# The ninth key block's low-half score term, made over the full array and ahead of the side-by-side pair

## The chip, the cores and the metric

The kernel runs on one core of a Trainium2 chip. The metric is the device time of one launch in microseconds, and a kernel's time is the median of several launches. The engines are named as the profile names them: PE is the matrix engine (PEld its weight loads, which can lie beside its matmuls), DVE the vector engine, ACT the scalar engine, POOL the general-purpose engine, and SP the engine that issues the DMAs. PSUM is the memory into which PE writes its sums.

## The reference

An attention whose queries are averaged in twos feeds a two-layer network. It is cut here to what matters:

```python
# q, k, v: (4, 8, 1152, 64); w_in: (512, 2048); w_out: (2048, 512)
q_pool = q.reshape(B, H, S // 2, 2, D).mean(axis=3)        # 576 queries a head
scores = 1 / sqrt(D) * q_pool @ k.transpose(0, 1, 3, 2)    # 576 x 1152
attn = softmax(scores)
a = attn @ v
x = a.transpose(0, 2, 1, 3).reshape(B * S // 2, H * D)     # 2304 x 512
h = x @ w_in
out = where(h > 0, h, exp(min(h, 0)) - 1) @ w_out          # 2304 x 512, float32
```

## The kernel before, in words

All products are made on PE in half precision, with every operand split into a high half and a low half, so that a product is a sum of terms: high by high, high by low, low by high.

The work goes by batch, and in a batch by four pairs of heads. A pair's queries come in nine steps: four tiles of 128 queries for each of the two heads, and one last step in which the 64 queries that are left of each head stand together (`st.h is None`). That makes 4 x 4 x 9 = 144 steps, 128 of the first kind and 16 of the last.

A step begins with its scores (`scores()`, lines 712 to 733): 128 queries against 1152 keys, written to the one PSUM buffer `s` of three banks. The keys of a head lie in `kT` as nine blocks of 128. In a block the partitions hold 64 rows of the one half of the keys and 64 rows of the other; in the even blocks of the first head the high half lies below, in the odd ones above, and in the second head the other way round. `keys[h]` groups them: entry 0 is four blocks (512 columns) with the high half in partitions 0 to 63, entry 1 is four blocks with the high half in partitions 64 to 127, and entry 2 is the ninth block alone (128 columns). The queries lie in `qT`: index 0 has the high half in both sets of 64 partitions, index 1 the low half in both sets.

The first three matmuls (line 721) take the high half of the queries against all 128 partitions, that is against both halves of the keys: 512, 512 and 128 columns. The next three (line 730) take the low half of the queries against the high half of the keys, and so use 64 rows of the array each: entry 0 on rows 0 to 63 and entry 1 on rows 64 to 127, which stand next to each other in the order and run side by side (the pair), and then the ninth block alone, on the 64 rows where its high half lies. In a last step each of the six is there twice, once for each head, with 64 query columns.

After the scores, DVE scales them, copies them out of PSUM and takes the smallest of each row (`biggest`, line 736); ACT takes the exponential (line 742); a reciprocal, the high half of the weights (line 761 on ACT or 753 on POOL) and their low half (line 756 on DVE) follow; a transposing DMA makes `pT` (line 781); and PE multiplies it with the values (lines 819 and 825). Since there is one buffer `s`, the first score matmul of a step waits until line 736 of the step before has read it.

Beside this run the splitting of inputs and weights and the network, whose matmuls are lines 933 and 1000. What stands where on an engine is set by a planner in the kernel (`Plan.run`), which goes through all tasks with a written price and a due time for each. The scores are one task with a written price of 950 (1100 for a last step); what the function does inside is not seen by the planner.

The low half of the queries is put into `qT` by two DMAs (`q_lo`, line 525), one for each set of 64 partitions; the copy of the high half into the upper set (`q_hi`, line 528) is a task that follows them, and the scores follow `q_hi`.

Of the kernel before, what the change touches and what calls it, by code (L numbers as in the profile page):

```python
# [226 lines left out]
def attention_moe_kernel(  # L227
# [9 lines left out]
    nc = tc.nc  # L237
# [85 lines left out]
    for b, s0, nt, lo in [(b, 0, 4, True) for b in range(0, B)]:  # L323
# [6 lines left out]
        while t0 < u.n:  # L330
            n = 256 if u.n - t0 != 320 else 320
# [6 lines left out]
    for u in units:  # L338
# [3 lines left out]
        for p in range(NP):  # L342
            pr = Rec()
# [345 lines left out]
    r = plan.add("DVE", 150.0, 0.0, wo_top, wo_max)  # L689
# [12 lines left out]
    def attention(st):  # L702
        u, pr = st.u, st.pr
        t0 = st.t0
        s, nm, ep = (plan.buf(*x) for x in (("s",), ("nm",), ETAGS[u.i]))
# [6 lines left out]
        def scores():  # L712
            jobs = [(h, slice(64 * h, 64 * h + 64)) for h in range(2)] if st.h is None else [(st.h, slice(0, 128))]
            j = 2 * u.nt if st.h is None else st.t + st.h * u.nt
            keys = {}
            for h, rows in jobs:
                kt = pr.kT.ap[:, h]
                keys[h] = [kt[:, h:8:2], kt[:, 1 - h:8:2], kt[:, 8:9]]
            for c, n in enumerate((512, 512, 128)):
                for h, rows in jobs:  # L720
                    nc.tensor.matmul(  # L721
                        s.ap[rows, c, 0:n], pr.qT.ap[:, 0, j, rows], keys[h][c],
                        start=True, stop=False, skip_group_check=True,
                    )
            for cs in ((0, 1), (2,)):
                for h, rows in jobs:
                    for c in cs:
                        r0, n = ((0, 512), (64, 512), (64 * h, 128))[c]
                        r = slice(r0, r0 + 64)
                        nc.tensor.matmul(  # L730
                            s.ap[rows, c, 0:n], pr.qT.ap[r, 1, j, rows], keys[h][c][r],
                            start=False, stop=True, skip_group_check=True,
                        )

        def biggest():
            nc.vector.tensor_scalar(  # L736
# [42 lines left out]
        def ptr():  # L779
            nc.sync.dma_start_transpose(  # L780
                out=pT.ap[:, :, half * 128:half * 128 + 128], in_=ep.ap[:, 0:2 * S]
            )

        ts_ = plan.add("PE", 950.0 if st.h is not None else 1100.0, t0 - K("KS", u), scores, pr.kdone + [pr.qs], [s, pr.kT, pr.qT])
        tm = plan.add("DVE", 1345.0, t0 - K("KM", u), biggest, [ts_, pr.sc], [s, nm, ep, pr.sm])
        te = plan.add("ACT", 1255.0, t0 - K("KE", u), expo, [tm], [nm, ep])
# [59 lines left out]
        n = 256 if st.h is not None else 128  # L846
# [217 lines left out]
```

## Time and profile before

| what | value |
|---|---|
| median of three runs | 947.41 us |
| lowest and highest run | 945.33 and 953.8 us |
| the profiled execution, its own time | 947.0 us |
| its span, first to last instruction | 945.2 us |
| mean granted clock of PE in it | 0.899 of full speed |
| busy PE, DVE, ACT, POOL | 740.6, 728.4, 691.2, 370.6 us |

The span is what the rows of the trace can explain; 1.8 us of the profiled execution lie around it. An engine's busy time is the time in which at least one of its instructions ran. Matmuls are pipelined: one starts while the one before it is still in the array, so what one costs the engine is the distance between starts, and its recorded length is longer. The ends of matmuls are modelled.

### The profile page before, as it was taken

Reading aid. Unit: us, or ns where it says so; the run is one execution under the profiler, and the core shown is the slowest. Engines: PE = TensorE matmul, PEld = TensorE weight load, DVE = VectorE, ACT = ScalarE, POOL = GpSimd, SP = SyncE. Lnnn points to the kernel's source line nnn. Section 1 sums busy time; section 2 is a strip of 40 time slices with the busy share of each in tenths; the row PEclk is TensorE's granted clock in tenths of the full one; section 3 lists DMA queues with packets and bytes.
Section 4 is the critical chain, followed back from the end, with each engine's and each line's share of the span. In section 5 each row is a group of like instructions: output and inputs, shape, how many; then the busy total and the mean of one; then the engine's idle time right before and its main releaser. Section 6 shows DMA issues by size and latency. Waiting matters only on the chain.

```text
span 945.2 us, 14736 instructions
## 1 busy us (share of the span) xinstructions
PE 740.6 (78%) x5283; PEld 420.6 (44%) x5283; DVE 728.4 (77%) x1235; ACT 691.2 (73%) x1169; POOL 370.6 (39%) x344
## 2 busy tenths in 40 slices
PE   0256555566939898988997989769979899789997
PEld 0123232233716455445644544338436544366563
DVE  5998999989898878867785897877877897785220
ACT  4587868878778879767777997568877987675360
POOL 3420513101737757402623772226324852034260
PEclk9998656657959999999998989989989999789999
DMA  7899999999948679897598989886799889754000
GB/s 235 221 211 199 232 224 250 237 188 263 224 95 182 133 166 207 153 185 125 110 186 183 196 172 208 160 160 105 158 212 202 170 157 173 133 100 76 23 1 28
DMA packets 434056, 156.94 MB, mean 166 GB/s; under 512 B 395840, under 2 KB 414272, under 8 KB 433984
## 3 DMA queue, kind: packets, MB, share of 16 engines
q1 hardware_dynamic: 433984, 156.01, 79.6%
q8 instruction: 41, 0.67, 0.3%
q14 instruction: 31, 0.25, 0.1%
HBM read 45.09 MB, written 4.72 MB: 53 GB/s over the span
## 4 chain that ended last, share of the span: by engine, by line
PE 28%; DVE 17%; DMA 14%; ACT 7%; issue 6%; POOL 5%; SPq 1%; DVEq 0%; POOLq 0%; ACTq 0%
DMA pT<-ep 11%; PE r L933 11%; PE r L1000 9%; DVE ep L736 6%; DVE ep L756 5%; PE r L819 3%; ACT ep L742 3%; PE s L721 2%; PE r L825 2%; POOL g L972 2%; PE s L730 1%; DMA kT<-kn 1%; DVE x L842 1%; ACT ep L761 1%; ACT tmp L944 1%
## 5 line engine op out<-in xcount | busy, mean ns | idle before, releaser
L756 DVE SCALAR_TENSOR_TENSOR ep<-ep,nm 128x1152 f16<-128x1152 f32 x132 | 209.7, 1593 | 18.1 <-ACT ep L761 10.5
L742 ACT ACTIVATE ep<-ep,nm 128x1152 f32<-128x1152 f32 x132 | 165.2, 1251 | 77.4 <-DVE ep L736 57.9
L736 DVE TENSOR_SCALAR_CACHE_REDUCE ep<-s,sm 128x1152 f32<-128x1152 f32 x132 | 186.3, 1411 | 40.6 <-DMA pT<-ep 25.7
L933 PE MATMUL r<-x,wi 128*128 128x256 f16 (+1 forms) x1536 | 204.1, 293 | 8.1 <-DVE x L842 4.2
L721 PE MATMUL s<-kT,qT 128*128 128x512 f16 (+3 forms) x480 | 108.8, 368 | 90.8 <-DVE ep L736 71.3
L933 PEld LDWEIGHTS <-wi 128*128 128x128 f16 x1536 | 150.5, 100 | 58.4 <-issue 18.3
L1000 PE MATMUL r<-wo,g 128*128 128x512 f16 (+1 forms) x864 | 174.4, 380 | 0.0
L761 ACT ACTIVATE ep<-ep,nm 128x1152 f16<-128x1152 f32 x111 | 138.3, 1247 | 23.7 <-DVE nm L750 23.3
L819 PE MATMUL r<-pT,v 128*128 128x256 f16 (+1 forms) x855 | 107.3, 281 | 31.1 <-DMA pT<-ep 16.5
L1000 PEld LDWEIGHTS <-g 128*128 128x128 f16 (+1 forms) x864 | 73.1, 100 | 87.9 <-issue 9.3
L949 POOL TENSOR_SCALAR tmp<-tmp,us 128x320 f32<-128x320 f32 (+1 forms) x96 | 73.2, 765 | 93.3 <-ACT tmp L944 92.9
L721 PEld LDWEIGHTS <-qT 128*128 128x128 f16 (+1 forms) x480 | 40.8, 105 | 144.5 <-issue 113.6
L819 PEld LDWEIGHTS <-v 128*128 128x128 f16 x864 | 72.5, 108 | 62.6 <-issue 33.1
L954 DVE SCALAR_TENSOR_TENSOR tmp<-r,wk,tmp 128x320 f32<-128x320 f32 (+1 forms) x96 | 57.5, 611 | 31.0 <-POOL tmp L949 30.6
L753 POOL TENSOR_SCALAR ep<-ep,nm 128x1152 f16<-128x1152 f32 x21 | 29.2, 1392 | 128.7 <-DVE nm L750 127.3
L972 POOL TENSOR_TENSOR g<-tmp,g 128x320 f16<-128x320 f32 (+1 forms) x70 | 72.1, 1036 | 12.0 <-ACT g L968 10.4
L730 PE MATMUL s<-kT,qT 64*128 64x512 f16 (+3 forms) x480 | 72.2, 369 | 0.0
L825 PE MATMUL r<-pT,v 128*64 128x256 f16 (+1 forms) x855 | 67.6, 282 | 0.0
L384 POOL TENSOR_SCALAR q<-q,sm 128x576 f32<-128x576 f32 x14 | 12.6, 897 | 134.6 <-ACT qn L429 119.2
L941 ACT ACTIVATE tmp<-r 128x320 f32<-128x320 f32 (+1 forms) x96 | 46.5, 485 | 24.4 <-PE r L933 19.6
L944 ACT ACTIVATE tmp<-tmp,us 128x320 f32<-128x320 f32 (+1 forms) x96 | 58.0, 608 | 1.3
L837 ACT ACTIVATE x<-r,sm 64x256 f32<-64x256 f32 (+1 forms) x96 | 39.8, 414 | 23.7 <-PE r L825 22.3
(123 smaller groups left out, 960.1 us busy)
## 6 DMA issues: line engine op xcount, KB each, us to landing
k<-in_k_dram SPq DMA_DIRECT2D x16, 576.0 KB, 5.0
v<-in_v_dram SPq DMA_DIRECT2D x16, 576.0 KB, 4.6
q<-in_q_dram SPq DMA_DIRECT2D x32, 256.0 KB, 3.4
qT<-qT SPq DMA_DIRECT2D x48, 144.0 KB, 2.8
g<-in_moe_w_in_dram SPq DMA_DIRECT2D x13, 512.0 KB, 5.6
g<-in_moe_w_out_dram SPq DMA_DIRECT2D x13, 512.0 KB, 5.2
out_dram<-tmp SPq DMA_DIRECT2D x16, 256.0 KB, 2.8
pT<-ep SPq DMA_TRANSPOSE x130, 4.8
```

The costliest lines, as they stand in the source:

```text
L721: nc.tensor.matmul(s.ap[rows, c, 0:n], pr.qT.ap[:, 0, j, rows], keys[h][c], start=True, stop=False, skip_group_check=True,)
L730: nc.tensor.matmul(s.ap[rows, c, 0:n], pr.qT.ap[r, 1, j, rows], keys[h][c][r], start=False, stop=True, skip_group_check=True,)
L736: nc.vector.tensor_scalar(e_(), s.ap.rearrange("p a b -> p (a b)")[:, 0:S], pr.sm.ap[:, 12:13], None, op0=ALU.mult, op1=ALU.min, accum_out ...
L742: nc.scalar.activation(out=e_(), in_=e_(), func=AF.Exp, bias=nm.ap[:, 0:1], scale=-1.0, accum_out=nm.ap[:, 2:3],)
L756: nc.vector.scalar_tensor_tensor(out=p_(1), in0=e_(), scalar=nm.ap[:, 3:4], in1=p_(0), op0=ALU.mult, op1=ALU.subtract)
L761: nc.scalar.activation(out=p_(0), in_=e_(), func=AF.Copy, scale=nm.ap[:, 3:4])
L819: nc.tensor.matmul(x.ap[:, os], vt[:, order[c]].rearrange("p e d -> p (e d)"), pT.ap[:, c, cs], start=(c == 0), stop=False, skip_group_che ...
L825: nc.tensor.matmul(x.ap[r0:r0 + 64, os], vt[:, order[c], 0], pT.ap[:, NCH + c, cs], start=False, stop=(c >= NCH - 2), skip_group_check=True,)
L933: nc.tensor.matmul(hp.ap[:, f * n:(f + 1) * n], w[:, a, c, (f0 + f) * 128:(f0 + f + 1) * 128], x16.ap[:, e, c, g0:g0 + n], start=(i == 0), ...
L949: nc.gpsimd.tensor_scalar(en.ap[:, :m], en.ap[:, :m], -1.0, us.ap[:, 5:6], op0=ALU.add, op1=ALU.mult)
L972: nc.gpsimd.tensor_tensor(out=l, in0=gv, in1=h, op=ALU.subtract)
L1000: nc.tensor.matmul(op.ap[r0:r0 + tn, :], gt[qd].ap[:, a, fi, o:o + tn], w_out16(f // 2)[:, e, f % 2, :], start=(i < 128 // tn), stop=(i >= ...
```

## The change

The ninth block's low-half term is taken out of the set of 64-row matmuls. It is now made over all 128 partitions, with the low half of the queries against both halves of the keys, and it stands between the three high-half matmuls and the pair. The term low by low is added by it for the ninth block alone. The pair is now the last of the group.

```diff
-            for cs in ((0, 1), (2,)):
-                for h, rows in jobs:
-                    for c in cs:
-                        r0, n = ((0, 512), (64, 512), (64 * h, 128))[c]
-                        r = slice(r0, r0 + 64)
-                        nc.tensor.matmul(
-                            s.ap[rows, c, 0:n], pr.qT.ap[r, 1, j, rows], keys[h][c][r],
-                            start=False, stop=True, skip_group_check=True,
-                        )
+            for h, rows in jobs:
+                nc.tensor.matmul(
+                    s.ap[rows, 2, 0:128], pr.qT.ap[:, 1, j, rows], keys[h][2],
+                    start=False, stop=True, skip_group_check=True,
+                )
+            for h, rows in jobs:
+                for c in range(2):
+                    r = slice(64 * c, 64 * c + 64)
+                    nc.tensor.matmul(
+                        s.ap[rows, c, 0:512], pr.qT.ap[r, 1, j, rows], keys[h][c][r],
+                        start=False, stop=True, skip_group_check=True,
+                    )
```

In the changed file the moved matmul is line 726 and the pair is line 733; later lines stand three further down (1000 is 1003).

On PE, a group in the middle of the run that a matmul of the second layer follows. `LDWEIGHTS` is a weight load, `MATMUL` names result, moving operand and weights, and the size at the end is that of the result. First before:

```order
L721 MATMUL s_3613<-kT_2455,qT_2444 128x128
L730 LDWEIGHTS qT_2444
L730 MATMUL s_3613<-kT_2455,qT_2444 128x512
L730 LDWEIGHTS qT_2444
L730 MATMUL s_3613<-kT_2455,qT_2444 128x512
L730 LDWEIGHTS qT_2444
L730 MATMUL s_3613<-kT_2455,qT_2444 128x128
L1000 LDWEIGHTS g_3017
L1000 MATMUL r_3385<-wo_1503,g_3017 128x512
```

The same place after:

```order
L721 MATMUL s_3613<-kT_2455,qT_2444 128x128
L726 LDWEIGHTS qT_2444
L726 MATMUL s_3613<-kT_2455,qT_2444 128x128
L733 LDWEIGHTS qT_2444
L733 MATMUL s_3613<-kT_2455,qT_2444 128x512
L733 LDWEIGHTS qT_2444
L733 MATMUL s_3613<-kT_2455,qT_2444 128x512
L1003 LDWEIGHTS g_3017
L1003 MATMUL r_3385<-wo_1503,g_3017 128x512
```

The 128-column matmul of the low half went from behind the pair to ahead of it; as many loads and matmuls as before stand there, and what precedes and follows the group is the same.

On PE, the first group of a pair of heads, with the semaphores on which an instruction waits (DMAHW4 and DMAHW5 belong to the two DMAs of `q_lo`). Before:

```order
L721 MATMUL s_228<-kT_169,qT_159 128x128
L730 LDWEIGHTS qT_159 [waits DMAHW4_49]
L730 MATMUL s_228<-kT_169,qT_159 128x512
L730 LDWEIGHTS qT_159 [waits DMAHW5_49]
L730 MATMUL s_228<-kT_169,qT_159 128x512
```

After:

```order
L721 MATMUL s_228<-kT_169,qT_159 128x128
L726 LDWEIGHTS qT_159 [waits DMAHW5_49,DMAHW4_49]
L726 MATMUL s_228<-kT_169,qT_159 128x128
L733 LDWEIGHTS qT_159
L733 MATMUL s_228<-kT_169,qT_159 128x512
```

Both waits now stand at the load of the moved matmul. On DVE, ACT, POOL and SP the order and the waits are the same in both kernels, and on PE nothing outside the groups moved.

## Rows read from the trace of the kernel before

**Rows 1.** The page's busy time, and the chain that ended last by engine and line.

```profile
PE 740.6 (78%) x5283; PEld 420.6 (44%) x5283; DVE 728.4 (77%) x1235; ACT 691.2 (73%) x1169; POOL 370.6 (39%) x344
...
PE 28%; DVE 17%; DMA 14%; ACT 7%; issue 6%; POOL 5%; SPq 1%; DVEq 0%; POOLq 0%; ACTq 0%
...
by line: DMA pT<-ep 10.6%; PE r L933 10.6%; PE r L1000 9.1%; issue 6.3%; DVE ep L736 5.5%; DVE ep L756 4.7%; PE r L819 2.9%; ACT ep L742 2.7%; PE s L721 2.3%; PE r L825 1.7%; POOL g L972 1.6%; PE s L730 1.4%; DMA kT<-kn 0.9%; DVE x L842 0.9
```

**Rows 2.** The page's costliest groups: busy us, mean ns | idle before, releaser.

```profile
L736 DVE TENSOR_SCALAR_CACHE_REDUCE ep<-s,sm 128x1152 f32<-128x1152 f32 x132 | 186.3, 1411 | 40.6 <-DMA pT<-ep 25.7
...
L721 PE MATMUL s<-kT,qT 128*128 128x512 f16 (+3 forms) x480 | 108.8, 368 | 90.8 <-DVE ep L736 71.3
...
L721 PEld LDWEIGHTS <-qT 128*128 128x128 f16 (+1 forms) x480 | 40.8, 105 | 144.5 <-issue 113.6
...
L730 PE MATMUL s<-kT,qT 64*128 64x512 f16 (+3 forms) x480 | 72.2, 369 | 0.0
```

**Rows 3.** The waits, whole span: us in total, times, longest us.

```profile
PE s L721 <- DVE ep L736: 71.3, 47, 10.8
...
PEld L730 <- issue: 45.1, 144, 0.5
...
DVE ep L736 <- PE s L730: 10.8, 12, 2.0
```

**Rows 4.** Timeline of PE, one group at full clock: start us, length us, instruction.

```profile
404.11 0.38 PE L721 MATMUL s<-kT,qT 128*128 128x512 f16 x1 [0.47 <-DVE ep L736]
404.32 0.38 PE L721 MATMUL s<-kT,qT 128*128 128x512 f16 x1
404.54 0.22 PE L721 MATMUL s<-kT,qT 128*128 128x128 f16 x1
404.69 0.39 PE L730 MATMUL s<-kT,qT 64*128 64x512 f16 x2
404.92 0.22 PE L730 MATMUL s<-kT,qT 64*128 64x128 f16 x1
405.06 0.39 PE L1000 MATMUL r<-wo,g 128*128 128x512 f16 x1
```

**Rows 5.** Timeline of PE, one full-array stream of 64 columns, and its weight loads.

```profile
257.56 0.44 PE L819 MATMUL r<-pT,v 128*128 128x64 f16 x9
257.92 0.34 PE L825 MATMUL r<-pT,v 128*64 128x64 f16 x9
...
257.56 0.32 PEld L819 LDWEIGHTS <-v 128*128 128x128 f16 x9
```

**Rows 6.** Timeline of PE: two side-by-side 512-column matmuls, then one over the full array.

```profile
423.05 0.38 PE L1000 MATMUL r<-wo,g 128*64 128x512 f16 x2
423.36 0.39 PE L721 MATMUL s<-kT,qT 128*128 128x512 f16 x1
```

**Rows 7.** Timeline of PE, the end of one last step's group.

```profile
417.53 0.41 PE L730 MATMUL s<-kT,qT 64*64 64x512 f16 x4
417.77 0.23 PE L730 MATMUL s<-kT,qT 64*64 64x128 f16 x2
417.93 0.28 PE L819 MATMUL r<-pT,v 128*128 128x256 f16 x1
```

**Rows 8.** Timeline of PE, the end of a group at half clock.

```profile
410.84 0.31 PE L721 MATMUL s<-kT,qT 128*128 128x128 f16 x1
411.08 0.61 PE L730 MATMUL s<-kT,qT 64*128 64x512 f16 x2
411.48 0.31 PE L730 MATMUL s<-kT,qT 64*128 64x128 f16 x1
411.73 0.39 PE L819 MATMUL r<-pT,v 128*128 128x256 f16 x1
```

**Rows 9.** Stretches of rows 4 and 8: busy by engine, then PE's granted clock, DMA.

```profile
404.10:405.06 0.96, 0.95 (x6) 0.31 (x6) 0.96 (x1) 0.96 (x1) 0.00 (x0) 1.00 1.37 157
410.03:411.73 1.70, 1.70 (x7) 0.39 (x6) 1.29 (x2) 1.62 (x3) 0.00 (x0) 0.50 0.65 122
```

## The prediction

> **What bounds the kernel now.** I read first the busy times: PE, DVE and ACT are each busy for about three quarters of the span and none is full, so no single engine sets the end [rows 1]. Then the chain that ended last: it runs through PE for 28% of the span, DVE 17%, DMA 14%, ACT 7%. The reader should look there for the lines that the change touches: score lines 721 and 730 hold 2.3% and 1.4%, together 3.7% of 945.2 us, or 35 us [rows 1]. Both lines together are busy for 108.8 + 72.2 = 181 us [rows 2]. So about a fifth (35 / 181 = 0.19) of the time in the score matmuls lies on the path that sets the end. That fifth is what I multiply PE's savings by, since in the other groups PE waits anyway: the waits show PE's line 721 standing 71.3 us for the DVE copy that frees the one PSUM buffer [rows 3]. In the other direction DVE's line 736 stands for the end of the low-half matmuls only 12 times, for 10.8 us in all [rows 3].
>
> Next comes the timeline of one group, because the whole change lies inside it. At full clock (granted 1.00 there [rows 9]) the starts are: two high-half matmuls of 512 columns at 404.11 and 404.32, the high half of the ninth block at 404.54, the pair at 404.69, the ninth block's low half at 404.92, and the second layer at 405.06 [rows 4]. Distances between starts are what counts. A 512-column matmul costs 0.215, so 128 columns should cost a quarter, 0.054. But from the 128-column matmul to the pair it is 0.15, and from the last 128-column matmul to the next full-array one 0.14. So going from the full array to 64 rows, and coming back, costs about 0.09 each time, on top of the columns.
>
> **The change part by part.** Loads and matmuls are as many as before, with the same numbers of columns: per group 512, 512, 128, a pair of 512, and 128. Entry into 64 rows and return from it happen once each, before and after. What moves is the second 128.
>
> Removed, per group of the first kind at full clock: the stretch from the pair to the short matmul (404.69 to 404.92, 0.23) and from it to the next work (0.14), together 0.37 [rows 4].
>
> Added: (a) a second full-array matmul of 128 columns behind the first. No row shows two in a row. Its price is bounded from below by 0.03: nine full-array matmuls of 64 columns have their loads within 0.32 us, and with the last load's own length of some 0.105 taken off, eight steps take 0.215 [rows 2, 5]. It is bounded from above by 0.15, the step at which the array changes its shape [rows 4]. I take 0.055, the quarter of a 512, since the 64-column stream shows that a full-array matmul with a load of its own is spaced by its columns. (b) The way from the pair straight to the next full-array work. No row shows that either; the nearest is two side-by-side 512s, split in columns of the array rather than in rows, followed by a full-array matmul: 423.05 to 423.36, 0.31 [rows 6]. The lower bound is 0.215, a return that costs nothing; the upper one 0.215 + 0.14 = 0.36, the columns plus the whole of today's last step. I take 0.31.
>
> Sum per group: 0.055 + 0.31 - 0.37 = about -0.005 us, which is within the rounding. In a last step, from the pairs to the short ones 0.24 and on to the next work 0.16 [rows 7], 0.40 in all, against 0.055 + 0.31 and 0.01 for the second head's start, is -0.02. At half clock (0.50 [rows 9]) it is 0.24 into the pair, 0.40 to the short matmul, 0.25 to the next work: 0.89 [rows 8]. Afterwards it is 0.11 for the second 128, 0.24, and then 0.40 or 0.43 (twice 0.215) with a return of 0.14 (0.25 less 0.11): 0.89 to 0.92, so 0.00 to +0.03 slower; I take +0.015. With two clock levels and a mean granted clock of 0.899, PE is at the lower for (1 - 0.899) / 0.5 = 20% of the time, hence about 29 of 144 groups. All together: 102 x -0.005 - 13 x 0.02 + 29 x 0.015 = -0.3 us of PE time, of which a fifth is on the path: **-0.1 us**.
>
> The release of DVE is the other thing that moves: `biggest` starts on the last matmul of the group, which was a short one and is now the second of the pair. Before: pair to short 0.23, and 0.22 for the short one's length, 0.45 behind the pair's start. After: the pair starts 0.055 later and lasts 0.39, 0.445 [rows 4]. The ends are modelled, so the difference of 0.005 is none; a matmul's columns plus its way through the array are the same in either order. So the loop of scores and copy does not get shorter.
>
> The waits for the two DMAs of the low half of the queries now both stand at the load of the moved matmul, and queued behind it are the pair and all of PE. In the trace of before the loads of line 730 never waited for a DMA, only for "issue" (45.1 us in 144 groups [rows 3]), and the first score matmul, ahead of them, already waits for a task that follows these two DMAs. I cost the merged wait at nothing; if its cover were gone, it would be 16 waits, one for each pair of heads.
>
> Other engines and queues keep their order, so nothing else moves but by these hundredths.
>
> **Bounds.** With both unknown prices at their upper ends a group costs 0.095 + 0.05 - 0.005 = +0.14, or 20 us of PE in 144 groups and 4 us on the path: 951.0. With both at the lower ends it costs -0.025 - 0.095 - 0.005 = -0.125, or -18 us and -3.6 us on the path: 943.4.
>
> **The rivals.** Slower: the load of the moved matmul is not hidden. The load of a full set of weights is recorded at 105 ns on average [rows 2], longer than the 54 ns of the 128-column matmul ahead of it, whereas it stands behind a pair of 512 today. If the second short matmul had to wait for its load, each group would cost 0.105 - 0.055 = +0.05 us, 7.2 us of PE, **948.4** with a fifth on the path and 954.2 with every group on it. Against it speak the 64-column matmuls, spaced at under 0.03 with loads just as long [rows 5]. It decides from the point where the two short starts lie more than 0.055 apart; over 1% it would need 0.066 per group and all groups on the path.
> The Trainium skill's page "TensorE: Matmul & The Clock Gate", section "LDWEIGHTS (loading the stationary operand)", speaks for this rival: a load takes as many nanoseconds as it has columns over 1.2, about 107 for a full set. By that as a spacing the sum would be the 948.4 above; the recorded length agrees, the spacing in rows 5 does not, so I keep this as a rival.
>
> Faster: the return from the pair costs nothing, because the next full-array work enters behind a long pair rather than behind a short matmul. Then each group saves 0.095, 13.7 us of PE, **944.3** with a fifth on the path, and over 1% faster only where 70% of the groups were on it. Against it speaks the 0.31 behind the side-by-side 512s, which has 0.095 over its columns [rows 6].
>
> Clock: the low half of the ninth block uses 128 rows instead of 64, and PE might be granted the full clock more often. If all of the fifth that runs at half clock went to full, half of 20% of PE's busy 740.6 us, 74 us, would go, 28% of it on the path, 21 us: **926**. The columns that go through PE and its gaps stay the same, so I see no ground for it.
>
> **How the numbers follow.** The forecast is the profiled execution's 947.0 us less 0.1; that execution lies 0.4 us under the median of 947.41, so **947.0** serves for both. Its chance is 0.81; the slower rival gets 0.09, the faster 0.07, the clock 0.03. The bounds of the prices give 943.4 to 951.0. The same program's runs lie from 945.33 to 953.8, two of the three within 2.1 us, so I widen each end by about 1: 942.5 to 952.0, which takes in the first two rivals as priced. A change of under 1% is about what a measurement of this kernel cannot tell from none. Over 1% faster takes most of the clock rival and the far end of the faster one, 0.05; over 1% slower the far end of the slower one and a clock that turns the other way, 0.05; within 1% is left with 0.90.
>
> **What would show it.** In the timeline of the changed kernel at full clock: the moved matmul 0.05 to 0.06 behind the ninth block's high half; the pair 0.15 behind that; the next full-array work 0.31 behind the pair. A distance of 0.10 between the short ones shows the load; 0.22 behind the pair shows a free return. The wait of DVE's line 736 for the score matmuls should stay near 11 us in a dozen times, the mean granted clock near 0.90, and the moved matmul's load should not wait for a DMA. The forecast is wrong if more than a fifth of the groups are on the path, or if shifts of hundredths change which transposing DMA is late, which no row here prices.

## The result, and the profile after

The changed kernel takes 940.9 us in the median (938.42 to 945.23, 10 runs), the kernel before on the same chip 950.72 us (942.96 to 953.8, 10 runs). The ratio is 0.9915, with a 95% interval from 0.989 to 0.994: faster by 0.85%, some 8 us. That is inside the band of 1% that got most of the chance, but the time is 1.6 us below the low end of the range, and the forecast of -0.1 us is not what happened.

The two profiled executions stand 947.0 against 944.64 us, so only 2.4 of the 8 us lie between them: the one of before is 3.7 us under its median here, the one after 3.7 us above its own. What they show well is the inside of a group, what stands where, and the time from the 45th group on, where traces of one kernel agree (table at the end of the experiments).

The page of the changed kernel, span, busy time and chain by engine:

```profile
span 942.8 us, 14748 instructions
...
PE 733.5 (78%) x5283; PEld 428.9 (45%) x5283; DVE 730.5 (77%) x1235; ACT 690.6 (73%) x1169; POOL 370.0 (39%) x344
...
PE 25%; DVE 17%; DMA 14%; ACT 8%; issue 7%; POOL 6%; SPq 2%; DVEq 0%; POOLq 0%; ACTq 0%
```

They answer to [rows 1]. As many matmuls as before, but twelve instructions more than the 14736 of before. PE's busy time is 7.1 us smaller.

The page's groups after (the copy is now line 739, the pair 733), which answer to [rows 2]:

```profile
L739 DVE TENSOR_SCALAR_CACHE_REDUCE ep<-s,sm 128x1152 f32<-128x1152 f32 x132 | 186.4, 1412 | 40.8 <-DMA pT<-ep 28.0
...
L721 PE MATMUL s<-kT,qT 128*128 128x512 f16 (+3 forms) x480 | 108.7, 368 | 91.9 <-DVE ep L739 73.6
```

The waits after, as in [rows 3]:

```profile
PE s L721 <- DVE ep L739: 73.6, 47, 10.8
...
DVE ep L739 <- PE s L733: 7.9, 9, 2.4
```

Neither the copy nor the score matmuls wait noticeably more or less. The timeline of PE after, for the group of [rows 4] from its second matmul on:

```profile
408.21 0.38 PE L721 MATMUL s<-kT,qT 128*128 128x512 f16 x1
408.42 0.22 PE L721 MATMUL s<-kT,qT 128*128 128x128 f16 x1
408.48 0.22 PE L726 MATMUL s<-kT,qT 128*128 128x128 f16 x1
408.63 0.39 PE L733 MATMUL s<-kT,qT 64*128 64x512 f16 x2
408.95 0.39 PE L1003 MATMUL r<-wo,g 128*128 128x512 f16 x1
```

The second 128 follows 0.06 behind the first (forecast 0.055), the pair 0.15 behind that (0.15), the next work 0.32 behind the pair (0.31). With these, a group costs 0.06 + 0.32 - 0.37 = +0.01 us. At half clock, by the starts of such groups in the same trace, the three distances are 0.11, 0.25 and 0.54, together about the 0.89 of before. A last step ends so, against [rows 7]:

```profile
417.91 0.22 PE L726 MATMUL s<-kT,qT 128*64 128x128 f16 x2
418.07 0.41 PE L733 MATMUL s<-kT,qT 64*64 64x512 f16 x4
418.41 0.28 PE L822 MATMUL r<-pT,v 128*128 128x256 f16 x1
```

So the groups are what was forecast, and the 8 us do not come from their length. The one other thing that the trace shows at the moved line is the twelve instructions:

```profile
L726 PEldq EVENT_SEMAPHORE  x12: 51/51/51, 39.2 to 783.5; - x12
```

These are instructions of 51 ns each in PE's queue, at loads where two waits now stand together; the order listed them as part of the load.

### The profile page after: what moved, and what is told of

The parts are those of the page before. It is cut to its first block, busy times and chain, and to the rows that moved or that the text cites. A ratio compares the mean times of both kernels' runs of the same rounds, so it can differ in the third digit from the quotient of the medians.

```text
span 942.8 us, 14748 instructions
## 1 busy us (share of the span) xinstructions
PE 733.5 (78%) x5283; PEld 428.9 (45%) x5283; DVE 730.5 (77%) x1235; ACT 690.6 (73%) x1169; POOL 370.0 (39%) x344
## 4 chain that ended last, share of the span: by engine, by line
PE 25%; DVE 17%; DMA 14%; ACT 8%; issue 7%; POOL 6%; SPq 2%; DVEq 0%; POOLq 0%; ACTq 0%
DMA pT<-ep 11%; PE r L936 9%; PE r L1003 8%; DVE ep L739 5%; DVE ep L759 4%; PE r L822 3%; ACT ep L745 3%; PE s L721 2%; PE r L828 2%; POOL g L975 1%; ACT ep L764 1%; DMA q<-in_q_dram 1%; PE s L733 1%; DMA kT<-kn 1%; DVE x L845 1%
## 5 line engine op out<-in xcount | busy, mean ns | idle before, releaser
L936 PE MATMUL r<-x,wi 128*128 128x256 f16 (+1 forms) x1536 | 200.6, 289 | 8.8 <-DVE x L845 4.8
L936 PEld LDWEIGHTS <-wi 128*128 128x128 f16 x1536 | 148.6, 99 | 55.5 <-issue 17.6
L822 PE MATMUL r<-pT,v 128*128 128x256 f16 (+1 forms) x855 | 104.8, 276 | 32.2 <-DMA pT<-ep 12.4
L828 PE MATMUL r<-pT,v 128*64 128x256 f16 (+1 forms) x855 | 65.7, 276 | 0.0
L733 PE MATMUL s<-kT,qT 64*128 64x512 f16 (+1 forms) x320 | 62.6, 435 | 0.0
L840 ACT ACTIVATE x<-r,sm 64x256 f32<-64x256 f32 (+1 forms) x96 | 39.8, 415 | 20.9 <-PE r L828 19.3
```

Source lines behind the costliest of these rows:

```text
L733: nc.tensor.matmul(s.ap[rows, c, 0:512], pr.qT.ap[r, 1, j, rows], keys[h][c][r], start=False, stop=True, skip_group_check=True,)
L822: nc.tensor.matmul(x.ap[:, os], vt[:, order[c]].rearrange("p e d -> p (e d)"), pT.ap[:, c, cs], start=(c == 0), stop=False, skip_group_che ...
L828: nc.tensor.matmul(x.ap[r0:r0 + 64, os], vt[:, order[c], 0], pT.ap[:, NCH + c, cs], start=False, stop=(c >= NCH - 2), skip_group_check=True,)
L936: nc.tensor.matmul(hp.ap[:, f * n:(f + 1) * n], w[:, a, c, (f0 + f) * 128:(f0 + f + 1) * 128], x16.ap[:, e, c, g0:g0 + n], start=(i == 0), ...
```

## The experiments

Ratios are to runs of the kernel before on the same chip, with 95% intervals; each kernel has 6 to 12 runs. The clock is the granted clock, the median of a kernel's runs.

**First four: the row count or the order?** At first I looked at the clock. In the trace after, PE was granted half clock for less time in the middle of the run, and the ten runs showed 0.902 to 0.918 against the 0.899 of the profile before. So one theory was that a short matmul over all 128 rows keeps PE at its full level; a rival, that the order does it; a third, that any small shift reshuffles the run.

*c_before*, the kernel before unchanged.

> The kernel before, unchanged, as a control. Every theory expects the ratio to the kernel before at 1.000 with the interval across it, a median near 950 us. What it gives is the granted clock of each of its runs: the clock theory (the short matmul over all 128 rows keeps PE at its full level for more of the time) expects 0.895 to 0.901 here, against 0.902 to 0.918 in the ten runs of the changed kernel. The theory that only the order counts, and the theory that any shift of hundredths reshuffles the run, expect no such separation, or none that goes with the time.

Measured: 0.9989 (0.9962 to 1.0016), 949.46 us, clock 0.900, from 0.890 to 0.907.

*e_full_last*, the short matmul over 128 rows, behind the pair:

```diff
-            (short matmul over 128 rows)
             (pair)
+            (short matmul over 128 rows)
```

> The short low-half matmul over all 128 rows, but behind the pair, where it stood before. Clock theory: the gain stays, ratio 0.988 to 0.995, clock 0.904 to 0.915. Order theory (what counts is that the pair is last and the short matmul ahead of it): no gain, ratio 0.997 to 1.003. Reshuffling theory: anything from 0.988 to 1.005, without relation to the clock. By starts alone the group should be as long as in the changed kernel, within 0.01 us.

Measured: 0.9978 (0.9958 to 0.9998), 949.3 us, clock 0.904.

*e_short64_first*, the short matmul ahead of the pair, on 64 rows:

```diff
+                r = slice(64 * h, 64 * h + 64)
-                    s.ap[rows, 2, 0:128], pr.qT.ap[:, 1, j, rows], keys[h][2],
+                    s.ap[rows, 2, 0:128], pr.qT.ap[r, 1, j, rows], keys[h][2][r],
```

> The short low-half matmul ahead of the pair, but on 64 rows as before, without the second key half. Order theory: the gain stays, ratio 0.988 to 0.995. Clock theory: no gain, ratio 0.997 to 1.003, clock near 0.90. Reshuffling theory: anything from 0.988 to 1.005. By starts alone the group is shorter by about 0.05 us, since the short matmul lies in the same shape of the array as the pair and its rows may run beside it.

Measured: 0.9998 (0.9976 to 1.0021), 950.87 us, clock 0.899.

*c_after*, the changed kernel again.

> The changed kernel once more, as a control on this chip: ratio 0.989 to 0.994 by every theory, clock 0.902 to 0.918.

Measured: 0.9916 (0.9894 to 0.9938), 943.31 us, clock 0.906.

The gain repeats, and neither half of the change has it. The order alone gives nothing. The full rows alone raise the clock by 0.004 and give at most 0.4%, so the clock theory as I had put it fell, unless a later release of DVE had eaten its gain in *e_full_last*.

**Next four: the merged wait, the clock, the release.** What only the changed kernel had was the pair of waits at one load.

*e_first_new*, the new form only in the first step of each pair of heads:

```diff
+            if st is pr.steps[0]:
+                (short matmul over 128 rows, then the pair)
+            else:
+                (the old three)
```

> The new form of the group in the first step of each pair of heads only (16 of 144 groups), the old form elsewhere. These 16 groups are those in which the two waits for the copies of the low half stand at one load. Wait theory (the merged wait, with the twelve extra semaphore instructions that it brought, moved the time): the whole gain, ratio 0.989 to 0.995. Clock theory (a short matmul over 128 rows in every group keeps PE longer at its full level): a ninth of the gain, 0.998 to 1.001, clock 0.898 to 0.902.

Measured: 0.9969 (0.9948 to 0.999), 946.32 us, clock 0.8985; 14748 instructions.

*e_first_old*, the same with the two branches exchanged.

> The complement: the old form in the first step of each pair, the new one in the other 128 groups. The waits stand as in the kernel before. Wait theory: no gain, 0.998 to 1.002. Clock theory: eight ninths of the gain, 0.990 to 0.995, clock 0.904 to 0.910.

Measured: 1.001 (0.9985 to 1.0034), 948.84 us, clock 0.905; 14736 instructions.

*e_old_fullextra*, one more short matmul over 128 rows:

```diff
+            for h, rows in jobs:
+                nc.tensor.matmul(
+                    s.ap[rows, 2, 128:256], pr.qT.ap[:, 0, j, rows], keys[h][2],
+                    start=True, stop=True, skip_group_check=True,
+                )
             for cs in ((0, 1), (2,)):
```

> The group of the kernel before, and one more matmul over 128 rows and 128 columns ahead of the pair, into columns of the buffer that nothing reads. The group and the release of DVE become about 0.055 us later, and the pair is not last. Clock theory: the clock rises to 0.904 to 0.912, half-clock time between 290 and 815 us falls from 41 to 51 to about 30 us, and the time falls in spite of the longer group, ratio 0.991 to 0.998. Theory that it takes the order and the rows together for another reason (what follows the pair): no gain, or a loss of 0.055 x 144 x a fifth, 1.6 us, ratio 1.000 to 1.004.

Measured: 1.0011 (0.9988 to 1.0033), 950.1 us, clock 0.908. The extra matmul opens a sum in the bank in which the ninth block's sum is still open, so the ninth block presumably keeps only its low-half term here, which no run shows apart.

*e_old_late*, one more matmul of 256 columns on 64 rows at the end of the group:

```diff
+                nc.tensor.matmul(
+                    s.ap[rows, 2, 128:384], pr.qT.ap[r, 1, j, rows], keys[h][0][r][:, 0:2],
+                    start=True, stop=True, skip_group_check=True,
+                )
```

> The group of the kernel before, and one more matmul of 256 columns on 64 rows at its end, into columns that nothing reads: DVE is released about 0.11 us later and the group is 0.11 us longer, and no row more of the array is used than before. It prices what the short full-array matmul behind the pair paid (its release was 0.11 us later than before, its clock 0.904, and its time the same as before). Clock theory: the late release costs what the clock gave there, so ratio 1.004 to 1.009 here and a clock near 0.90. Theory that the clock is worth nothing: the release is worth nothing either, ratio 0.999 to 1.003; the fifth on the path of the prediction would give 3 us, 1.003.

Measured: 1.0022 (0.9995 to 1.0048), 949.22 us, clock 0.907.

The new form in 128 of 144 groups gives nothing, although its clock is up; in the 16 groups with the merged wait it gives 0.3%, which neither theory's range holds. That pointed to the twelve instructions, without showing them to be enough. The clock theory missed in *e_old_fullextra*, which got its clock and no gain, and in *e_old_late*, whose clock rose with 64-row columns alone. These last two don't price the clock or the release cleanly, because each adds 320 instructions, which the next four show to be a change of its own.

**Last four: the groups whole, the program longer.** The merged wait shows only its 51 ns, so I asked whether it acts by its length in PE's program. The groups stay whole here; matmuls whose result nothing reads are put at the very start, where PE has no work for 11 us:

```diff
     with tc.manual_schedule():
+        lead = ps.tile([128, 3, 512], F32, tag="s0", name="s0")
+        i16 = ident.bitcast(F16)
+        for _ in range(20):
+            nc.tensor.matmul(lead[:, 2, 128:192], i16[:, 0:128], i16[:, 0:64], start=True, stop=True, skip_group_check=True)
         plan.emit()
```

*e_old_lead12*, six of them in the kernel before.

> The kernel before with six small matmuls (twelve instructions) at the very start of PE's program, where PE stands idle for 11 us, into the PSUM buffer before its first use. All groups are as in the kernel before; every instruction of PE behind them lies twelve places later in its program. Place theory (what moved the time is where PE's instructions lie relative to the pieces in which its program is fetched by the instruction queue, since the fetches share the DMA engines with the transposing DMAs; the changed kernel has twelve more instructions): the time moves, by as much as 0.9% in either direction, and the fetches shift against the groups. Theory that the form of the groups makes the gain: ratio 0.998 to 1.002.

Measured: 0.9955 (0.9928 to 0.9983), 945.46 us, clock 0.903. By the profile's count this kernel has 11 instructions more than before, and the next two 39 and 127: one semaphore instruction fewer stands behind the leading matmuls.

*e_old_lead40*, twenty.

> The same with twenty small matmuls, forty places. Place theory: a ratio that differs from that of twelve places and of none by more than the interval, anywhere from 0.989 to 1.006. Form theory: 0.998 to 1.002.

Measured: **0.9913** (0.9879 to 0.9948), 941.43 us, clock 0.9035. This is the whole gain of the change, in a kernel whose score groups are those of before. The interval overlaps that of *e_old_lead12*, so the two are not told apart, though the place theory expected that they would be.

*e_old_lead128*, sixty-four.

> The same with 64 small matmuls, 128 places, half of the distance between two fetches as the trace has them (41 fetches for some 10,436 instructions, about 255 each). Place theory: the largest shift, a ratio from 0.989 to 1.006 that differs from the others. Form theory: 0.998 to 1.002.

Measured: 0.9997 (0.9973 to 1.0021), 949.65 us, clock 0.8755. The place theory expected its largest shift here, and there is none. The clock is lower at the start: in its trace PE is granted 0.68 up to the 45th group, against 0.78 before.

*e_new_lead128*, sixty-four in the changed kernel.

> The changed kernel with the same 64 small matmuls at the start. Place theory: the gain goes or halves, ratio 0.994 to 1.004, as its fetches now fall elsewhere. Form theory: the gain stays, 0.989 to 0.994, and then the shape, the order and the merged wait together make it.

Measured: 0.9982 (0.9954 to 1.0011), 949.35 us, clock 0.8785. The gain of the change is gone. The low clock is not the reason: the five runs at 0.898 to 0.911 have a median of 949.46 us, the seven at 0.864 to 0.882 one of 947.33.

The page of *e_old_lead40*, span and one group:

```profile
span 939.7 us, 14775 instructions
...
L730 PE MATMUL s<-kT,qT 64*128 64x512 f16 (+3 forms) x480 | 71.9, 369 | 0.0
```

Line 730 is busy for 71.9 us against 72.2 in [rows 2]: the groups are the same, and the span is 5.5 us shorter.

**How the places could act.** PE's program is fetched through a queue of its own, q8, while the kernel runs: it has 41 packets here, 42 with the 64 leading matmuls, and 43 in *e_old_late* with 320 instructions more. The DMA queues in the page of the changed kernel, packets, MB and share of 16 engines:

```profile
q1 hardware_dynamic: 433984, 156.01, 81.0%
q8 instruction: 41, 0.67, 0.3%
```

41 packets of 0.67 MB are 16 KB each; from the first to the last of them PE starts about 255 instructions to a packet. In this trace such a packet holds a DMA engine for 0.9 to 1.7 us, 0.96 in the median. All 16 engines also carry the transposing DMAs that make `pT`. Where a packet falls follows how many instructions PE has taken: between traces with equally many PE instructions, the instruction that PE has reached at a fetch differs by 2 to 4 in the median, from before to after by 13, to *e_old_lead12* by 12 and to *e_old_lead40* by 25.

Take one transposing DMA, the 49th of a run. In the kernel before (the DMA's issue, count and us to landing, then the queue in the 0.2 us in which the fetch starts, 346.5 to 346.7; the share is of 16 engines' time in that stretch):

```profile
pT<-ep SPq DMA_TRANSPOSE x1, 6.4
...
q8 instruction: 1, 0.02, 29.0%
```

It was issued at 342.2 us and the fetch came at 346.6, toward its end. In the changed kernel (queue from 348.1 to 348.3):

```profile
pT<-ep SPq DMA_TRANSPOSE x1, 5.5
...
q8 instruction: 1, 0.02, 37.4%
```

Issued at 346.8, the fetch at 348.2, 1.4 us in. In *e_new_lead128* no fetch meets it:

```profile
pT<-ep SPq DMA_TRANSPOSE x1, 4.5
```

The same DMA in seven runs, with starts and landings taken from the trace:

| kernel | fetch starts behind the issue by | issue to landing |
|---|---|---|
| before / c_before | 4.3 / 4.3 us | 6.38 / 6.34 us |
| after / c_after | 1.4 / 1.1 us | 5.51 / 5.44 us |
| e_old_lead12 | 1.1 us | 5.42 us |
| e_old_lead40 | -0.4 us | 5.56 us |
| e_new_lead128 | none | 4.55 us |

The other seven traces fit: met after 4.1 to 4.4 us it took 6.2 to 6.4 (*e_short64_first*, *e_full_last*, *e_first_old*), after 1.1 us 5.2 (*e_first_new*), and met by none 4.54 (*e_old_fullextra*, *e_old_late*, *e_old_lead128*).

Over the seven traces of the table I took every transposing DMA that makes `pT`, from the 21st on, that a fetch met, against the median of the same DMA in the traces where none met it, if these were two or more. Those met in their second half were longer by 1.4 us in the median (59 cases), those met in their first half by 0.46 us (96 cases).

Here DVE waits for this landing. Its timeline in the kernel before and then in the changed one, in the same stretch:

```profile
348.75 1.42 DVE L736 TENSOR_SCALAR_CACHE_REDUCE ep<-s,sm 128x1152 f32<-128x1152 f32 x1 [2.12 <-DMA pT<-ep]
```

```profile
352.44 1.42 DVE L739 TENSOR_SCALAR_CACHE_REDUCE ep<-s,sm 128x1152 f32<-128x1152 f32 x1 [1.25 <-DMA pT<-ep]
```

The stall is 0.87 us shorter, as the DMA is. The stretches around it, from the start of the 53rd group to that of the 57th, and from the 65th to the 69th, in all traces (worked out from the starts of line 721):

| kernel | ratio | 53rd to 57th | 65th to 69th |
|---|---|---|---|
| before / c_before | 1 / 0.9989 | 20.1 / 20.1 us | 19.3 / 17.3 us |
| e_short64_first | 0.9998 | 20.1 | 18.1 |
| e_full_last | 0.9978 | 20.1 | 17.7 |
| e_first_old | 1.001 | 20.1 | 19.1 |
| e_new_lead128 | 0.9982 | 20.2 | 17.5 |
| e_old_fullextra | 1.0011 | 19.9 | 17.1 |
| e_old_late | 1.0022 | 19.2 | 16.8 |
| e_old_lead128 | 0.9997 | 19.3 | 17.2 |
| e_first_new | 0.9969 | 19.0 | 15.6 |
| e_old_lead12 | 0.9955 | 19.0 | 15.5 |
| after / c_after | 0.9915 / 0.9916 | 19.1 / 19.0 | 15.9 / 15.9 |
| e_old_lead40 | 0.9913 | 19.1 | 16.9 |

The five kernels whose PE program has as many instructions as that of before (the first five names) all take 20.1 us in the first stretch, whatever the form of their groups. So the form doesn't sort this stretch, and the places in the program do. In *e_new_lead128* and *e_old_fullextra*, whose 49th DMA is met by no fetch, the 51st is, and takes 6.3 and 6.1 us, against 4.6 before. The second stretch is less sure, since two traces of the same kernel differ there by 2 us. Two stretches are not the whole, either: *e_old_late* and *e_old_lead128* gain here and lose elsewhere, and between the rows of before and after stand 2.5 to 4.5 of the 8 us.

The Trainium skill's page "Runtime: NRT & Kernel Launch", section "Instruction fetch mechanics", says that the program comes in blocks of 16 KiB, 256 instructions, through a DMA queue of the engine's own, and that crossing a boundary is mostly hidden. Size and count agree with the trace. Whether it is hidden for PE no run here shows; a transposing DMA that a block met landed later, by up to 1.8 us in the case above.

**What the whole run shows.** From the start of the 45th group to the end the traces show nearly the whole gain; before it they lie between 295.6 and 303.2 us, and the two of before differ there by 6.4 us. The last column is DVE's wait for the transposing DMAs at the copy, over the whole span, as in these rows of before, after, *e_old_lead40* and *e_new_lead128*:

```profile
DVE ep L736 <- DMA pT<-ep: 25.7, 26, 2.6
```

```profile
DVE ep L739 <- DMA pT<-ep: 28.0, 31, 2.5
```

```profile
DVE ep L736 <- DMA pT<-ep: 27.6, 28, 2.7
```

```profile
DVE ep L739 <- DMA pT<-ep: 36.3, 32, 2.6
```

| kernel | 45th group to the end | clock, 45th to 144th group | DVE's wait |
|---|---|---|---|
| before / c_before | 648.4 / 649.4 us | 0.95 / 0.94 | 25.7 / 27.5 us |
| e_first_old | 648.7 | 0.96 | 26.2 |
| e_new_lead128 | 649.5 | 0.96 | 36.3 |
| e_old_lead12 | 646.6 | 0.95 | 30.8 |
| e_first_new | 642.2 | 0.96 | 27.2 |
| after / c_after | 641.7 / 642.9 | 0.97 / 0.96 | 28.0 / 26.4 |
| e_old_lead40 | 640.5 | 0.97 | 27.6 |

The gain is not in that wait: it is no shorter in the fast kernels. Nor do the fetches lengthen the transposing DMAs by less there. Added up from the 21st DMA on, against the median of the same DMA where no fetch met it in the fourteen traces, it is 30.1 and 30.5 us in before and *c_before*, 30.6 and 29.9 in after and *c_after*, 30.4 in *e_old_lead40*. The loss in *e_new_lead128* does show: 36.2 us, and DVE waits 8.3 us longer than in the changed kernel. So fetches that meet transposing DMAs may explain why the gain went; how it came they do not explain by their sum. The clock is highest in the fast kernels, but *e_first_old* and *e_new_lead128* have 0.96 without a gain.

## Why the prediction was right or wrong

**The groups: right.** The second 128 at 0.055, its load hidden, the return from the pair at 0.31: measured 0.06, 0.15 and 0.32. Both rivals that hung on these fell by the same rows: the load is not exposed (that would have been 0.105), the return is not free (0.215). The ends were right too (0.06 + 0.39 = 0.45 behind the old start of the pair, as before), and DVE's wait for the group went from 12 times and 10.8 us to 9 times and 7.9 us.

**The clock: priced low, and it does not go with the time.** Kernels with a full short matmul in most groups show a median clock of 0.904 to 0.908 against 0.900, those with leading matmuls set aside. But *e_old_late*, which adds columns on 64 rows only, has 0.907, and *e_old_lead40*, with the groups of before, 0.9035, so the rows are not shown to raise it. *e_first_old* and *e_full_last* had a raised clock with ratios of 1.001 and 0.9978, and *e_first_new* is faster with 0.8985. So a higher clock alone does not make the 8 us. Whether it has a part in them is open.

**The step that failed** is the last of the part on the change: "Other engines and queues keep their order, so nothing else moves but by these hundredths", together with "I cost the merged wait at nothing". The wait itself shows only 51 ns twelve times. But merging two waits put twelve instructions more into PE's program, and with them the fetches of the program moved against the work. That instructions ahead of the old groups can make the whole gain is what *e_old_lead40* shows, with 0.9913. The page of before lists the instruction queue with 0.3% of the engines' time, and I took that for nothing. The last sentence of the prediction named the outcome, a change in which transposing DMA is late, but not that added instructions could do it with the groups as they are, and it gave it no price.

**The range.** A price for it could have come only from moving the program and measuring: kernels that are alike in their groups then ranged from 0.9913 to 0.9997. The 4.5 us below the forecast that I allowed were drawn from the matmuls' prices, and 8 us were needed. That the time still fell inside the band of 1% owes nothing to the sum.

**What stays open.** That idle matmuls at the start make the gain in the old kernel and take it away in the changed one is shown by *e_old_lead40* and *e_new_lead128*. That they act by the place of the program, and not by working PE at the start, is argued: the gain lies behind the 45th group, some 300 us later, but no run tried the one apart from the other. That a fetch lengthens the transposing DMA it meets is shown in one place by fourteen traces and by the medians above; that this makes the 8 us is not shown, and the sums speak against it unless it matters which of the DMAs are met. Nor do the places decide alone: *e_first_new* has as many instructions as the changed kernel, its fetches stand within 3 instructions of the changed kernel's in the median, and its ratio is 0.9969 with an interval that does not meet the other's. Its trace is as short as the changed kernel's from the 45th group on, so the rest may lie ahead of that, or in the form of the other 128 groups; no run separates these.

## What to carry to other kernels

In a kernel with some ten thousand instructions on one engine and a busy DMA path, a gain or loss under 1% may come from instructions added anywhere ahead, not from what the edit does. Before such an edit is credited, put a few idle instructions ahead of the old kernel's program, at two or three lengths, and see how far its time moves by that alone. Two waits that fall on one instruction can add an instruction, so compare the profile's instruction counts and not only the order.

## What the runs showed of the hardware that was not expected

A fetch of 16 KB of program, about 1 us of one DMA engine, lengthened a transposing DMA of 4.55 us to 5.2 to 5.6 us when it came early and to 6.2 to 6.4 us when it came near the end. Of the same kernel, twelve, forty and 128 instructions more at the start gave ratios of 0.9955, 0.9913 and 0.9997, so the effect does not grow with the number; in the changed kernel 128 took the gain away. A short matmul over 128 rows behind the pair (*e_full_last*) starts 0.32 us behind it and the next full-array work follows 0.07 us later: the way back to the full array is then paid inside the group, and the ratio is 0.9978 (0.9958 to 0.9998).
